# Moving the sums and splits of a third product's weights beside the second product

## The chip, the cores and the metric

One core of a Trainium2 chip runs the kernel, written by hand slot by slot. The metric is device microseconds of one execution (median of the runs shown).

## The reference, cut to what matters

All data are float32. Attention within chunks of 64 tokens makes `x` (4608 x 512); two expert blocks follow, each a product into 2048 columns, an elementwise function and a product back to 512:

```
x = chunked_attention(q, k, v)                      # 4608 x 512
g = relu(x @ w_in1) ** 2;  y = g @ w_out1           # products 1 and 2
h = y @ w_in2
g = where(h >= 1, h, where(h <= -1, 0, (h + 1) ** 2 / 4))   # product 3
out = g @ w_out2                                    # product 4
```

## The kernel before, in words

The weight inputs are 64-bit floats, read as pairs of 32-bit words and decoded to float32 in the kernel. Every operand of a product is split into a high part (a cast to float32r) and a low part (the rest), and each product is three matmuls: high x high, low x high, high x low. Products 2, 3 and 4 and the last part of product 1 use a seven-product scheme (P1 to P7) instead of eight block products. So each weight unit needs: decoding, four sums (`sums`) that turn 4 blocks into 7, a cast (high) and a subtraction (low), after which both are stored to DRAM buffers (`wd`) and loaded later product by product (`load_w`).

The order of all work is written out in slots. A slot is six matmuls of TensorE (PE); `pe_slot` puts matmuls, `at_slot` puts everything else behind them. All engines work through their own instructions in that order, and nearly all DMAs are issued by SyncE (SP) in that order too, so an issue that has to wait holds up all later ones. The stages are: slots 0 to 224 (SX) product 1 of seven of nine token blocks (`plain_h`) with the attention and the weight decoding beside it; slots 224 to 280 (SB1) the last two blocks as seven products (`form_p`); 280 to 560 (SA2) product 2 over five token pairs of 56 slots (`form_b`, w=0); 560 to 840 product 3 (`form_a`); then product 4.

Weight units: 48 units (three matrices m = 0, 1, 2 for products 2, 3 and 4, 16 units each), one begun every 97/20 = 4.85 slots from slot 28 (U0). `stage_unit` loads 512 KB into one of three buffers, `unit_a` (bits, lines 120 to 135) and `unit_b` decode: one ACT and four DVE instructions. For m = 0 and 1 `sums` follows on POOL (4 instructions, line 258), `unit_c` casts on ACT (line 283, tile `wh`, two buffers), `unit_hi` stores, `unit_d` subtracts on DVE (line 292, tile `wl`, two buffers) and stores. For m = 2 the decoded 256 KB go to DRAM (`wq`) and `late_a` to `late_d` load, sum, cast and subtract them beside product 3, 4 units in each pair but the last.

`pair_sums(i)` (line 201, four POOL instructions), `pair_hi` (ACT, line 218) and `pair_lo` (DVE, line 223) do the same for the eight weight pieces that `form_p` uses. `plain_end` squares a result tile `g` of product 1 on POOL (line 619) or ACT and stores it (line 625); `form_p` has four `g` buffers, written by ACT or DVE (line 775). In `form_p`, product P4 of a piece adds onto the bank that DVE reads for P7 (line 775), so its matmuls wait for that read.

Product 2 reads its activations back by `load_g` (line 807, four operands i = 0 to 3 of four parts kp), casts them on ACT (`prep_b`, line 639), subtracts on DVE (line 642) and combines operands on DVE (line 646), 5 slots ahead of PE, with three operand buffers.

Of the kernel before, what the change touches and what calls it, by code (L numbers as in the profile page):

```python
# [8 lines left out]
F32 = mybir.dt.float32  # L9
F32R = mybir.dt.float32r  # L10
U32 = mybir.dt.uint32
AF = mybir.ActivationFunctionType
ALU = mybir.AluOpType
AX = mybir.AxisListType

P = 128
# [18 lines left out]
def chunk_attention_moe_moe2(ctx, tc, q, k, v, w_in1, w_out1, w_in2, w_out2, out):  # L35
# [10 lines left out]
    nc = tc.nc  # L46
# [11 lines left out]
    BLK = 512  # L58
# [3 lines left out]
    NBL = len(blocks)  # L62
# [10 lines left out]
    def f(ap):  # L73
        return ap.bitcast(F32)
# [5 lines left out]
    def qt(tag, shape, dt, name):  # L80

        pool = mp if tag < NQM else late if tag < NQL else mid
        return pool.tile(shape, dt, tag=f"q{tag}", name=name, padded_shape=[P, 2, BLK])

    def ot(tag, n, name):

# [16 lines left out]
        for j in range(NPAIR) for dh in range(2) for th in range(2)  # L103
    }

    wd = {(m, a): dram.tile([P, 2, 2, 7, P], F32, name=f"w{m}_{a}") for m in range(3) for a in range(8)}

    wq = {(a, b): dram.tile([P, 4, P], F32, name=f"q{a}_{b}") for a in range(8) for b in range(2)}

# [151 lines left out]

    def unit_b(m, a, b):
        y, ab = wst[m, a, b]
        if m == 2:
            c = eu.tile([P, 4, P], F32, tag="wl", name="wq", bufs=2, padded_shape=[P, 7, P])
        else:
            c = eu.tile([P, 7, P], F32, tag="wc", name="wc", bufs=1)
        nc.vector.scalar_tensor_tensor(  # L270
            out=c[:, 0:4].rearrange("p a f -> p (a f)"), in0=ab, scalar=TINY, in1=f(y), op0=ALU.is_ge, op1=ALU.mult
        )
        wst[m, a, b] = c
        if m == 2:
            nc.sync.dma_start(out=wq[a, b], in_=c[:, 0:4])
            del wst[m, a, b]
        else:
            sums(c)

    def unit_c(*u):  # L280
        c = wst[u]
        hi = eu.tile([P, 7, P], F32R, tag="wh", name="wh", bufs=2)
        nc.scalar.copy(hi, c)
        wst[u] = (c, hi)

    def unit_hi(m, a, b):
        nc.sync.dma_start(out=wd[m, a][:, 0, b], in_=f(wst[m, a, b][1]))

    def unit_d(m, a, b):
        c, hi = wst.pop((m, a, b))  # L290
        lo = eu.tile([P, 7, P], F32R, tag="wl", name="wl", bufs=2)
        nc.vector.tensor_tensor(out=lo, in0=c, in1=f(hi), op=ALU.subtract)
        nc.sync.dma_start(out=wd[m, a][:, 1, b], in_=f(lo))


    def late_a(a, b):
        c = mp.tile([P, 7, P], F32, tag=f"q{LATE[0]}", name="lc", padded_shape=[P, 8, P])
        nc.sync.dma_start(out=c[:, 0:4], in_=wq[a, b])
        wst[a, b] = c

    def late_b(a, b):
        sums(wst[a, b])

    def late_c(a, b):
        c = wst[a, b]
        hi = mp.tile([P, 7, P], F32R, tag=f"q{LATE[1]}", name="lh", padded_shape=[P, 8, P])
        nc.scalar.copy(hi, c)
        wst[a, b] = (c, hi)

    def late_d(a, b):  # L310
        c, hi = wst.pop((a, b))
        nc.gpsimd.tensor_tensor(out=c, in0=c, in1=f(hi), op=ALU.subtract)
        store_parts(2, a, b, hi, c)

    wt, wv = {}, {}

    def load_w(m, tag, a, prod):
        if tag < 3 * NF:
            t = wp.tile([P, 2, 2, P], F32R, tag=f"w{tag}", name=f"w{m}")
        else:  # L320
            if tag % 2 == 0:
                wv[tag // 2] = wp.tile([P, 2, 2, 2, P], F32R, tag=f"v{tag // 2 - 3 * NF // 2}", name=f"w{m}")
            t = wv[tag // 2][:, tag % 2]
        nc.sync.dma_start(out=f(t), in_=wd[m, a][:, :, :, CIDX[prod]])
        wt[m, a, prod] = t

# [286 lines left out]
    def plain_end(j, fi, g, own):  # L615
        if own:
            nc.scalar.square(g, g)
        else:
            nc.gpsimd.tensor_tensor(out=g, in0=g, in1=g, op=ALU.mult)  # L619
        kh, kk = divmod(fi, HF)  # L620
        b0, n = blocks[j]
        for p, th, t0, m in halves:
            lo, hi = max(b0, t0), min(b0 + n, t0 + m)
            if lo < hi:
                nc.sync.dma_start(out=gd[0, p, kh, th, kk // 2][:, kk % 2, lo - t0:hi - t0], in_=g[:, lo - b0:hi - b0])  # L625
# [305 lines left out]
    with tc.manual_schedule():  # L931
# [150 lines left out]

        units = [(m, a, b) for m in range(3) for a in range(8) for b in range(2)]
        for n, u in enumerate(units):
            g = U0 + n * 97 // 20
            if n < NWS:
                at_slot(U0 - 4 + n, stage_unit, *u)
            at_slot(g, unit_a, *u)
            if n + NWS < len(units):
                at_slot(g, stage_unit, *units[n + NWS])  # L1090
            at_slot(g + 2, unit_b, *u)
            if u[0] < 2:
                at_slot(g + 4, unit_c, *u)
                at_slot(g + 5, unit_hi, *u)
                at_slot(g + 6, unit_d, *u)
        done = g + 7
        assert done <= SB1 - 16, done

# [15 lines left out]


        for i in range(HF):
            s = 165 + 14 * i if i < 3 else SX + 7 * (i - 3) + 7
            at_slot(s, pair_sums, i)
            at_slot(s + 3, pair_hi, i)
            at_slot(s + 4, pair_lo, i)  # L1120
            for prod, o in OFFS.items():
                pe_slot(SX + 7 * i + o, form_p, i, prod)
        m = mid_at
# [39 lines left out]
        for w, s0 in ((0, SB1), (1, SB2)):  # L1163
            for j in range(NPAIR):
                for r, prod in enumerate(RANK):
                    s = s0 + 56 * j + 8 * r
                    for kk in range(HF):
                        pe_slot(s + kk, form_b, w, j, prod, kk)
                    for kp in range(HF // 2):
                        t = s + ((0, 2, 1, 3)[kp] if ended(w, j, prod) else 2 * kp) - PREP  # L1170
                        if j == 0 and r == 0 and w == 0:
                            t = max(t, done + 12)
                        at_slot(t, prep_b, w, j, prod, kp)
                        if prod in AFTER:
                            at_slot(t + 3, comb_b, w, j, prod, kp)
                        if j + 1 < NPAIR:

                            for i, p, d in ((0, "P2", 3), (1, "P3", 3), (3, "P7", 0), (2, "P4", 0)):
                                if p == prod:
                                    at_slot(t + d, load_g, w, j + 1, i, kp)  # L1180
        for kp in range(4):
# [10 lines left out]
        for j in range(NPAIR):  # L1192
            if j == 0:
                e = SA2
                loads = tuple(e - 24 + n for n in range(4))
                times = dict(P1=e - 18, P5=e - 13, P6=e - 8, P3=e - 1, P2=e, P7=e + 1, P4=e + 5)
                combs = (("P1", e - 16, 0), ("P5", e - 11, 0), ("P1", e - 2, 1), ("P2", e + 3, 0))
            else:
                b = SA2 + 7 * (HF * j - 1)
                l0 = SA2 + 7 * (HF * (j - 1) + 2)  # L1200
                loads = tuple(l0 + 7 * n for n in (0, 1, 3, 2))
                times = dict(P1=b - 8, P5=b + 1, P6=b + 5, P3=b + 4, P2=b + 6, P7=b + 7, P4=b + 11)
                combs = (("P1", b - 6, 0), ("P1", b - 5, 1), ("P5", b + 2, 0), ("P2", b + 9, 0))
            for i in range(4):
                at_slot(loads[i], load_xa, j, i, A_RAW[i])
            for prod in sorted(ORD, key=times.get):
                at_slot(times[prod], prep_a, j, prod)
                at_slot(times[prod] + 1, rest_a, j, prod)
            for prod, t, n in combs:
                at_slot(t, comb_a, j, prod, n)  # L1210
            if j + 1 < NPAIR:
                for n in range(4):
                    g = SA2 + 56 * j + 12 + 13 * n
                    u = divmod(4 * j + n, 2)
                    for d, fn in ((0, late_a), (4, late_b), (8, late_c), (9, late_d)):
                        at_slot(g + d, fn, *u)


        for t in range(56):
            r, kk = divmod(t, 8)  # L1220
            i, ro = divmod(t, 7)

            tag = (t + 2 * NF) % 56
            if t < 32:
                s = SX + (23, 30, 37, 44, 51, 58, 65, 45, 9, 11, 16, 18, 30, 44, 58, 29)[t // 2] + t % 2 - 2 * (t < 4)
            else:
                s = SB1 + t - 30
            at_slot(s, load_w, 0, tag, kk, RANK[r])
            two = int(tag >= 3 * NF and tag % 2 == 0)
            at_slot(SB1 + 56 * (NPAIR - 1) + t + t // 2 + two, load_w, 1, tag, i, ORD[ro])  # L1230
            i, ro = divmod(t + two, 7)
            at_slot(SA2 + 7 * (HF * (NPAIR - 1) + i) + OFFS[ORD[ro]] + t // 2, load_w, 2, tag, kk, RANK[r])

        l = SA2 + 7 * (HF * NPAIR - 1)
        for kp in range(4):
# [53 lines left out]
```

## Time and profile before

| | us |
|---|---|
| median of 3 runs | 1589.98 (1589.93 to 1598.41) |
| the profiled execution | 1592.96 |
| its span, first to last instruction | 1591.2 |
| PE busy | 1540.8 (97%) |
| DVE, ACT, POOL busy | 1144.5, 880.1, 337.5 |
| DMA queue of SP | 341.46 MB, 70.9% of 16 engines' span |

The span is what the chain of instructions takes; 1.8 us lie around it. Busy shares are averages over stages with different limits, so a stage is read from the stretch of time in which it runs: `plain_h` until about 440 us, `form_p` until about 538 us, product 2 until about 900 us, product 3 until about 1240 us. PE wait rows say what ended a wait; the granted clock (PEclk) is 1.00 at 2.4 GHz and 0.50 at 1.2 GHz.

### The profile page before, as it was taken

The numbers are of one execution on the slowest core, as the hardware profiler recorded it, in microseconds if no ns is written. First come the engines' busy times: TensorE is split into PE (matmuls) and PEld (weight loads), VectorE is DVE, ScalarE is ACT, GpSimd is POOL, SyncE is SP. The second block draws the span as 40 slices with busy tenths as digits, with TensorE's granted clock in tenths as the row PEclk, the third lists the DMA queues.
The fourth block names the chain that finished last, engine by engine and source line by source line (L and its number), as shares of the span: only waits on it lengthen the run. The fifth ranks groups of instructions, "written<-read, shape, count | busy, mean of one in ns | idle before, by whom it ended". The sixth has DMA issues, their size and how long they took to land.

```text
span 1591.2 us, 26749 instructions
## 1 busy us (share of the span) xinstructions
PE 1540.8 (97%) x9456; PEld 1352.1 (85%) x9456; DVE 1144.5 (72%) x1448; ACT 880.1 (55%) x1785; POOL 337.5 (21%) x382
## 2 busy tenths in 40 slices
PE   7999999989989789999999999999999999999998
PEld 5788888777867668999999888999999889999998
DVE  7977687666696647777776857677575787878876
ACT  6877777666543334444444567667675544444442
POOL 0145555565457200000000022223220000000000
PEclk9999999999999989999999999999999999999999
DMA  9989999999868975336175785655769983744633
GB/s 221 243 269 310 294 294 304 294 298 302 284 194 257 338 218 175 105 127 193 56 241 163 237 295 188 230 189 197 241 219 307 341 220 74 198 112 120 169 75 47
DMA packets 445606, 343.63 MB, mean 216 GB/s; under 512 B 209952, under 2 KB 414752, under 8 KB 445472
## 3 DMA queue, kind: packets, MB, share of 16 engines
q1 hardware_dynamic: 441760, 341.46, 70.9%
q8 instruction: 75, 1.23, 0.3%
q10 hardware_dynamic: 3712, 0.46, 0.2%
q14 instruction: 59, 0.48, 0.1%
HBM read 197.13 MB, written 144.70 MB: 215 GB/s over the span
## 4 chain that ended last, share of the span: by engine, by line
PE 83%; DMA 6%; DVE 4%; issue 2%; SPq 2%; ACT 2%; POOL 2%; POOLq 0%; DVEq 0%; ACTq 0%
PE X L652 37%; PE V L652 18%; PE ph L596 12%; PE W L652 9%; DMA w<-w 2%; PE psA L408 2%; DMA w<-wl 1%; DMA g<-g 1%; PE X L756 1%; PE psD L518 1%; PE psB L431 1%; POOL g L619 1%; PE psC L486 1%; ACT s L449 1%; SPq L625 1%
## 5 line engine op out<-in xcount | busy, mean ns | idle before, releaser
L652 PE MATMUL X<-oh,w 128*128 128x448 f32 (+1 forms) x1920 | 549.0, 367 | 0.0
L639 ACT CAST oh<-gr 128x896 fp32r<-128x896 f32 (+1 forms) x280 | 270.0, 964 | 336.4 <-PE X L652 148.6
L642 DVE TENSOR_TENSOR ol<-gr,oh 128x896 fp32r<-128x896 f32 (+1 forms) x280 | 312.4, 1117 | 166.9 <-ACT oh L639 160.8
L652 PEld LDWEIGHTS X<-oh,w 128*128 128x128 f32 x1920 | 360.1, 188 | 35.8
L652 PE MATMUL X<-ol,w 128*128 128x448 f32 (+1 forms) x960 | 353.2, 368 | 0.4 <-DVE ol L642 0.4
L652 PE MATMUL V<-oh,w 128*128 128x448 f32 (+1 forms) x960 | 276.3, 369 | 12.1 <-DMA w<-w 12.1
L619 POOL TENSOR_TENSOR g<-g 128x512 f32<-128x512 f32 x136 | 169.1, 1247 | 231.4 <-ACT g L608 190.2
L652 PEld LDWEIGHTS V<-oh,w 128*128 128x128 f32 x960 | 180.9, 189 | 31.0 <-issue 11.1
L652 PEld LDWEIGHTS X<-ol,w 128*128 128x128 f32 x960 | 180.1, 188 | 16.7 <-DVE ol L642 0.8
L596 PE MATMUL ph<-xh,ih 128*128 128x512 f32 x448 | 181.6, 405 | 0.0
L646 DVE TENSOR_TENSOR gr<-gr,gr 128x896 f32<-128x896 f32 (+1 forms) x160 | 179.4, 1121 | 1.7 <-DMA gr<-g 1.7
L652 PE MATMUL V<-ol,w 128*128 128x448 f32 (+1 forms) x480 | 177.3, 369 | 0.0
L596 PE MATMUL ph<-xh,il 128*128 128x512 f32 x448 | 175.4, 392 | 1.0 <-DVE il L189 1.0
L596 PE MATMUL ph<-xl,ih 128*128 128x512 f32 x448 | 175.8, 392 | 0.0
L258 POOL TENSOR_TENSOR lc<-lc 128x128 f32<-128x128 f32 x64 | 34.1, 543 | 506.4 <-DMA lc<-q 492.1
L652 PE MATMUL W<-oh,w 128*128 128x448 f32 (+1 forms) x480 | 137.2, 367 | 0.0
L789 ACT ACTIVATE t<-c,half 128x448 f32<-128x448 f32 (+1 forms) x120 | 81.2, 681 | 50.7 <-DVE c L712 49.8
L596 PEld LDWEIGHTS ph<-xl,ih 128*128 128x128 f32 x448 | 84.4, 188 | 18.3
L596 PEld LDWEIGHTS ph<-xh,il 128*128 128x128 f32 x448 | 84.8, 189 | 17.0 <-DVE il L189 1.4
L596 PEld LDWEIGHTS ph<-xh,ih 128*128 128x128 f32 x448 | 84.6, 189 | 16.0 <-ACT g L608 0.5
L652 PEld LDWEIGHTS W<-oh,w 128*128 128x128 f32 x480 | 90.0, 187 | 8.9
L652 PEld LDWEIGHTS V<-ol,w 128*128 128x128 f32 x480 | 90.6, 189 | 8.1
(116 smaller groups left out, 2043.5 us busy)
## 6 DMA issues: line engine op xcount, KB each, us to landing
gr<-g SPq DMA_DIRECT2D x128, 448.0 KB, 4.7
w<-w SPq DMA_DIRECT2D x168, 256.0 KB, 5.1
g<-t SPq DMA_DIRECT2D x128, 224.0 KB, 3.1
wu<-in_moe_w_out_dram SPq DMA_DIRECT2D x64, 256.0 KB, 4.7
gr<-g SPq DMA_DIRECT2D x32, 512.0 KB, 7.0
w<-wh SPq DMA_DIRECT2D x32, 448.0 KB, 4.5
w<-wl SPq DMA_DIRECT2D x32, 448.0 KB, 5.1
ws<-in_moe_w_in_dram SPq DMA_DIRECT2D x16, 512.0 KB, 4.6
```

The lines of the kernel that those rows point to most:

```text
L258: nc.gpsimd.tensor_tensor(out=c[:, o], in0=c[:, x], in1=c[:, z], op=op)
L408: nc.tensor.transpose(pt[:, h // HU, h // 2 % NP, :], qks[t][i][:, h:h + 2, :].rearrange("p h d -> p (h d)"), ident)
L431: nc.tensor.matmul(pt[rows(p), e, c * CH:(c + 1) * CH], qkT[rows(e), 0, p, rows(c)], qkT[rows(e), 1, p, rows(c)], start=True, stop=True,)
L449: nc.scalar.activation(out=s[:, e, c], in_=sc[:, e, c], func=AF.Exp, bias=m[:, e, c:c + 1], accum_out=z[:, e, c:c + 1],)
L486: nc.tensor.transpose(pt[:, e].rearrange("k p t -> k (p t)"), s[:, e, 2 * n:2 * n + 2].rearrange("q c k -> q (c k)"), ident)
L596: nc.tensor.matmul(ph, win[fi][wi][:, kt * P:(kt + 1) * P], x[:, i, :], start=(kt == 0 and a == 0), stop=(kt == KT - 1 and a == 2),)
L619: nc.gpsimd.tensor_tensor(out=g, in0=g, in1=g, op=ALU.mult)
L639: nc.scalar.copy(t[0], raw)
L642: nc.vector.tensor_tensor(out=t[1], in0=raw, in1=f(t[0]), op=ALU.subtract)
L646: eng.tensor_tensor(out=o, in0=x, in1=z, op=ALU.subtract)
L652: nc.tensor.matmul(o, wt_[:, wi, c, :], x[:, i, :], start=first and a == 0, stop=last and a == 2, skip_group_check=True,)
L789: nc.scalar.activation(out=t, in_=h, func=AF.Square, bias=half, scale=0.5)
```

## The change

Seven edits. (1) `unit_b` stops at the decoded blocks for m = 1 too and stores them to `wq`; sums, cast and subtraction become a `late_unit` beside pairs 0 to 3 of product 2, on tiles q16 to q21, q0 and q1 (those of operands 3 and 2 of `load_g`). (2) The loads of operands 3 and 2 for the next pair go 22 slots later in product 2. (3) Units of m = 0 begin every 5 slots, the other 32 every 4.25; the last ends at slot 246 instead of 262, and the first loads of operands 0 and 1, tied to that end, move with it. (4) For m = 0 high and low parts stand side by side in one tile and one DRAM buffer: one store of 896 KB instead of two, and `load_w` reads runs of 1024 instead of 512 bytes. (5) All `pair_sums` are made at slots 112 to 161; casts and subtractions come 3 slots earlier for i >= 3. (6) A `g` tile's store is issued 1 slot (2 in `form_p`) after its square instead of right behind it. (7) The subtraction and the stores of a late unit are separate steps.

```diff
     def unit_b(m, a, b):
-        if m == 2:
-            c = eu.tile([P, 4, P], F32, tag="wl", name="wq", bufs=2, padded_shape=[P, 7, P])
+        if m:
+            c = eu.tile([P, 4, P], F32, tag="wh", name="wq", bufs=2, padded_shape=[P, 14, P])
...
-        if m == 2:
-            nc.sync.dma_start(out=wq[a, b], in_=c[:, 0:4])
+        if m:
+            nc.sync.dma_start(out=wq[m, a, b], in_=c[:, 0:4])
...
     def unit_c(*u):
         c = wst[u]
-        hi = eu.tile([P, 7, P], F32R, tag="wh", name="wh", bufs=2)
+        w = eu.tile([P, 7, 2, P], F32R, tag="wh", name="wh", bufs=2)
+        nc.scalar.copy(w[:, :, 0], c)
...
+    def unit_d(m, a, b):
+        c, w = wst[m, a, b]
+        nc.vector.tensor_tensor(out=w[:, :, 1], in0=c, in1=f(w[:, :, 0]), op=ALU.subtract)
+
+    def unit_e(m, a, b):
+        nc.sync.dma_start(out=wd[m, a][:, b], in_=f(wst.pop((m, a, b))[1]))
...
+    def late_unit(s, u, tags, steps):
+        for d, fn, *args in zip(steps, (late_a, late_b, late_c, late_d, late_e), ((tags,), (), (tags,), (), ())):
+            at_slot(s + d, fn, *u, *args[0])
...
             nc.gpsimd.tensor_tensor(out=g, in0=g, in1=g, op=ALU.mult)
+        at_slot(cur[0] + (2 if j >= NBL - 2 else 1), plain_out, j, fi, g)
...
-            g = U0 + n * 97 // 20
+            g = U0 + 5 * n if n < 16 else U0 + 80 + (n - 16) * 17 // 4
...
-            s = 165 + 14 * i if i < 3 else SX + 7 * (i - 3) + 7
-            at_slot(s, pair_sums, i)
-            at_slot(s + 3, pair_hi, i)
-            at_slot(s + 4, pair_lo, i)
+            s = 166 + 12 * i if i < 3 else SX + 7 * (i - 3) + 7
+            at_slot(112 + 7 * i, pair_sums, i)
+            at_slot(s, pair_hi, i)
+            at_slot(s + 1, pair_lo, i)
...
-                            for i, p, d in ((0, "P2", 3), (1, "P3", 3), (3, "P7", 0), (2, "P4", 0)):
+                            for i, p, d in ((0, "P2", 3), (1, "P3", 3), (3, "P7", 0 if w else 22), (2, "P4", 0 if w else 22)):
...
+        for j in range(4):
+            for n, (d, tags) in enumerate(((29, (16, 17)), (33, (18, 19)), (45, (0, 1)), (49, (20, 21)))):
+                late_unit(SB1 + 56 * j + d, (1, *divmod(4 * j + n, 2)), tags, (0, 5, 8, 9, 11))
```

## Rows read from the trace of the kernel before

**Rows 1.** The page, part 1: busy time of each engine over the span.

```profile
...
PE 1540.8 (97%) x9456; PEld 1352.1 (85%) x9456; DVE 1144.5 (72%) x1448; ACT 880.1 (55%) x1785; POOL 337.5 (21%) x382
...
```

**Rows 2.** Stretches: us, PE, PEld, DVE, ACT, POOL busy, PEclk, DMA share, GB/s.

```profile
...
110.00:300.00 190.00, 189.97 (x1933) 156.96 (x1932) 141.54 (x213) 138.58 (x454) 111.69 (x141) 1.00 0.99 301
300.00:400.00 100.00, 91.14 (x907) 74.81 (x907) 64.49 (x92) 65.27 (x212) 58.29 (x69) 0.97 1.00 299
...
440.00:480.00 40.00, 33.92 (x138) 26.16 (x137) 36.70 (x42) 17.69 (x29) 25.78 (x22) 0.96 0.62 192
480.00:520.00 40.00, 37.25 (x156) 30.06 (x155) 24.30 (x28) 12.57 (x22) 28.43 (x28) 0.96 0.83 261
520.00:540.00 20.00, 15.84 (x64) 12.69 (x63) 10.62 (x10) 6.84 (x9) 8.78 (x6) 0.91 1.00 329
540.00:570.00 30.00, 17.87 (x69) 13.96 (x68) 13.04 (x11) 7.32 (x8) 0.24 (x1) 0.83 1.07 325
...
615.00:683.00 68.00, 68.00 (x335) 62.48 (x335) 49.31 (x50) 30.57 (x36) 0.00 (x0) 1.00 0.42 135
...
920.00:1240.00 320.00, 320.00 (x1571) 294.08 (x1570) 211.53 (x307) 214.00 (x345) 67.78 (x76) 1.00 0.69 234
...
```

**Rows 3.** Waits of PE from 300 to 400 us: total us, times, longest.

```profile
...
PE psD L518 <- ACT atT L505: 4.9, 1, 4.9
PE psC L486 <- ACT g L608: 1.5, 1, 1.5
PE psD L518 <- DMA vt<-in_v_dram: 1.5, 1, 1.5
PE psC L486 <- DVE s L460: 1.0, 1, 1.0
```

**Rows 4.** Waits of PE from 440 to 540 us.

```profile
...
PE X L756 <- DVE g L775: 10.6, 6, 4.2
PE X L756 <- DVE pl L744: 2.0, 1, 2.0
...
```

**Rows 5.** Waits of PE from 540 to 570 us.

```profile
...
PE V L652 <- DMA w<-w: 12.1, 2, 10.7
```

**Rows 6.** Chain that ended last, 525 to 570 us: start, length, what.

```profile
...
529.29 4.81 DMA g<-g
...
534.25 0.70 DVE g L775
...
537.93 8.24 PE X L652 x36
...
558.48 5.41 DMA w<-w
...
```

**Rows 7.** Timeline of ACT, 338.5 to 346 us: start, length, instruction [idle before].

```profile
...
341.70 0.94 ACT L283 CAST wh<-wc 128x896 fp32r<-128x896 f32 x1 [3.46 <-DMA w<-wh]
...
```

**Rows 8.** Groups of POOL, 245 to 520 us: xcount | busy us, mean ns | idle.

```profile
...
L201 POOL TENSOR_TENSOR iy<-iy,iy 128x256 f32<-128x256 f32 x16 | 15.1, 942 | 1.3
...
```

**Rows 9.** Timeline of SP (DMA issues), 530 to 572 us.

```profile
...
541.11 0.42 SPq L807 DMA_DIRECT2D gr<-g  x1
...
550.69 22.21 SPq L324 DMA_DIRECT2D w<-w  x20
```

**Rows 10.** Groups of POOL, 920 to 1240 us.

```profile
...
L312 POOL TENSOR_TENSOR lc<-lc,lh 128x896 f32<-128x896 f32 x16 | 35.5, 2218 | 65.1 <-ACT lh L307 65.1
L258 POOL TENSOR_TENSOR lc<-lc 128x128 f32<-128x128 f32 x60 | 32.3, 549 | 129.2 <-DMA lc<-q 115.0 <-DMA w<-w 11.8
```

**Rows 11.** DMA issues of the whole span: KB each, median us to landing.

```profile
...
gr<-g SPq DMA_DIRECT2D x128, 448.0 KB, 4.7
...
lc<-q SPq DMA_DIRECT2D x16, 256.0 KB, 4.2
...
```

**Rows 12.** The page, part 5: the splitting casts of ACT.

```profile
...
L639 ACT CAST oh<-gr 128x896 fp32r<-128x896 f32 (+1 forms) x280 | 270.0, 964 | 336.4 <-PE X L652 148.6
...
```

**Rows 13.** Line 642 on DVE, 920 to 1240 us: durations ns min/median/max.

```profile
...
L642 DVE TENSOR_TENSOR ol<-xr,oh x28: 1074/1090/1443, 953.1 to 1180.9; 128x896 fp32r<-128x896 f32 x28
...
```

More of the change, by code (lines that the diff above doesn't have):

```diff
@@ L82, in qt @@
         pool = mp if tag < NQM else late if tag < NQL else mid
-        return pool.tile(shape, dt, tag=f"q{tag}", name=name, padded_shape=[P, 2, BLK])
+        return pool.tile(shape, dt, tag=f"q{tag}", name=name, padded_shape=[P, 8, P] if shape[1] == 7 else [P, 2, BLK])
     def ot(tag, n, name):
@@ L104, in chunk_attention_moe_moe2 @@
     }
-    wd = {(m, a): dram.tile([P, 2, 2, 7, P], F32, name=f"w{m}_{a}") for m in range(3) for a in range(8)}
-    wq = {(a, b): dram.tile([P, 4, P], F32, name=f"q{a}_{b}") for a in range(8) for b in range(2)}
+    wd = {
+        (m, a): dram.tile([P, 2, 2, 7, P] if m else [P, 2, 7, 2, P], F32, name=f"w{m}_{a}")
+        for m in range(3) for a in range(8)
+    }
+    wq = {(m, a, b): dram.tile([P, 4, P], F32, name=f"q{m}_{a}_{b}") for m in (1, 2) for a in range(8) for b in range(2)}
     win = {}
@@ L281, in unit_c, with late_a, late_b, late_c @@
         c = wst[u]
-        hi = eu.tile([P, 7, P], F32R, tag="wh", name="wh", bufs=2)
-        nc.scalar.copy(hi, c)
[L284 to L311, printed above, removed]
-        nc.gpsimd.tensor_tensor(out=c, in0=c, in1=f(hi), op=ALU.subtract)
-        store_parts(2, a, b, hi, c)
+        w = eu.tile([P, 7, 2, P], F32R, tag="wh", name="wh", bufs=2)
+        nc.scalar.copy(w[:, :, 0], c)
+        wst[u] = (c, w)
+    def unit_d(m, a, b):
[3 more added lines that the diff above has]
+        nc.sync.dma_start(out=wd[m, a][:, b], in_=f(wst.pop((m, a, b))[1]))
+    def late_a(m, a, b, tags):
+        c = qt(tags[0], [P, 7, P], F32, "lc")
+        nc.sync.dma_start(out=c[:, 0:4], in_=wq[m, a, b])
+        wst[m, a, b] = c
+    def late_b(*u):
+        sums(wst[u])
+    def late_c(m, a, b, tags):
+        c = wst[m, a, b]
+        hi = qt(tags[1], [P, 7, P], F32R, "lh")
+        nc.scalar.copy(hi, c)
+        wst[m, a, b] = (c, hi)
+    def late_d(*u):
+        c, hi = wst[u]
+        nc.gpsimd.tensor_tensor(out=c, in0=c, in1=f(hi), op=ALU.subtract)
+    def late_e(*u):
+        c, hi = wst.pop(u)
+        store_parts(*u, hi, c)
+    def late_unit(s, u, tags, steps):
+        for d, fn, *args in zip(steps, (late_a, late_b, late_c, late_d, late_e), ((tags,), (), (tags,), (), ())):
+            at_slot(s + d, fn, *u, *args[0])
     wt, wv = {}, {}
@@ L323, in load_w @@
             t = wv[tag // 2][:, tag % 2]
-        nc.sync.dma_start(out=f(t), in_=wd[m, a][:, :, :, CIDX[prod]])
-        wt[m, a, prod] = t
+        c = CIDX[prod]
+        nc.sync.dma_start(out=f(t), in_=wd[m, a][:, :, :, c] if m else wd[m, a][:, :, c])
+        wt[m, a, prod] = t if m else t.rearrange("p b h f -> p h b f")
     att, ttile = {}, {}
@@ L619, in plain_end, with plain_out @@
             nc.gpsimd.tensor_tensor(out=g, in0=g, in1=g, op=ALU.mult)
+        at_slot(cur[0] + (2 if j >= NBL - 2 else 1), plain_out, j, fi, g)
+    def plain_out(j, fi, g):
         kh, kk = divmod(fi, HF)
@@ L1091, in chunk_attention_moe_moe2 @@
             at_slot(g + 2, unit_b, *u)
-            if u[0] < 2:
+            if u[0] == 0:
                 at_slot(g + 4, unit_c, *u)
-                at_slot(g + 5, unit_hi, *u)
                 at_slot(g + 6, unit_d, *u)
+                at_slot(g + 7, unit_e, *u)
         done = g + 7
@@ L1214, in chunk_attention_moe_moe2 @@
                     u = divmod(4 * j + n, 2)
-                    for d, fn in ((0, late_a), (4, late_b), (8, late_c), (9, late_d)):
-                        at_slot(g + d, fn, *u)
+                    late_unit(g, (2, *u), LATE, (0, 4, 8, 9, 9))
         for t in range(56):
```

## The prediction

> **What bounds the kernel now.** First the page's busy times: PE is busy 1540.8 us of a span of 1591.2 [rows 1], so 50.4 us of idle time, and what the lower clock costs, are all that a change beside the matmuls can win. Next the stretches [rows 2], to see where the idle time lies: PE is full from 110 to 300 us, from 615 to 683 and from 920 to 1240. It is idle 100 − 91.14 = 8.9 us between 300 and 400, and (40 − 33.92) + (40 − 37.25) + (20 − 15.84) + (30 − 17.87) = 25.1 us between 440 and 570. The remaining 16 us are the start and the tail, which the change does not touch. In the same rows PEclk falls to 0.97, 0.96, 0.96, 0.91 and 0.83: after some waits PE ran at 1.2 instead of 2.4 GHz. Each stretch times (1 − PEclk) gives 3.0, 1.6, 1.6, 1.8 and 5.1 us; where a long wait covers part of it (first and last) I count 2 and 2.5. So 34.0 us of waits and 9.5 us of clock, 43.5 us, is the most to be had. Last the waits themselves [rows 3 to 5] and who made them late.
>
> **Term 1, 300 to 400 us: 10.9 us (8.9 + 2).** The DMA engines are at a share of 1.00 here, as from 110 on at 0.99 [rows 2]. The longest wait, 4.9 us, ends with an ACT copy [rows 3]. ACT had stood 3.46 us before the cast `wh`, until the store of an earlier `wh` had landed [rows 7], with pair sums on POOL following (an instruction of theirs takes 0.94 us, [rows 8], four to a piece). Both leave this stretch. From unit 16 (slot 108) a unit brought 512 KB in and 896 KB out every 4.85 slots, 290 KB per slot; after the change it brings 512 in and 256 out every 4.25 slots, 181 KB per slot. In this stage that is 16 x 640 KB = 10.5 MB less, 35 us of DMA time at the 299 GB/s of the row. Nothing is added to ACT or DVE here, and pair sums take the POOL time that 16 x 4 sums leave. I take 10 won, 0.9 left (bounds: 7, if the three short waits of 4.0 us stay, to 10.9).
>
> **Term 2, the start of `form_p`: 3.6 us (2.0 + 1.6).** PE waits 2.0 us for the low part of P6 [rows 4] and then runs slow. DVE is busy 36.70 of 40 us there [rows 2], and closer units bring no relief: begun before at slots 226, 231, 236, 241, 246, now at 227, 231, 235, 239. What helps is only that operands land earlier when the DMA queue is emptier. Bounds 0 to 3.6; I take 1.6, nearer to nothing.
>
> **Term 3, P4 inside `form_p`: 8.0 us.** Six waits for DVE's read of P7 make 10.6 us [rows 4]; one is term 4 (4.2), 6.4 remain, and one half-speed stretch adds 1.6. DVE came late since POOL did the sums of a piece between squares, ACT's cast and DVE's subtraction waited for the sums, and the `g` stores behind waited on SP. Now sums are long done, ACT and DVE find their input ready, and units end at slot 246, a third of the way into the stage, instead of 262. I take 6.9 won, the first wait staying (bounds 3, if DVE is still full for half the stage, to 8.0).
>
> **Term 4, the last P4: 6.0 us (4.2 + 1.8).** The chain has a `g` store of 4.81 us landing at 534.1, DVE at 534.25, then PE [rows 6]: a store late in a queue with a share of 1.00 [rows 2]. Eight loads of 512 KB (operands 0 and 1) and the last units go about 16 slots earlier, out of this stretch. Against it: a store is now issued 2 slots, 2.7 us, later, and four buffers come round in 7 slots, 9.6 us (36 matmuls take 8.24 us [rows 6], a slot 1.37). The store's way is then 2.7 us + about 2 us of square and issue (estimate) + 3 to 4 us of landing, still under 9.6. I take 5.4 won (bounds 0 to 6.0).
>
> **Term 5, P5's weights in product 2: 14.6 us (12.1 + 2.5).** PE waits for a `load_w` [rows 5] issued 558.48 and landed 563.89 [rows 6]. It is P5's fifth weight: issue slot 289, use slot 292, with eight more 512 KB loads and eleven weight loads before it, and these do not move. The queue starts with the third part of operand 3, issued 541.11 [rows 9]: 3.2 us after the last P4 ended at 537.93 [rows 6], because the store of that P4 stood before it on SP. Now that store comes 2 slots later; ahead stands only the one of P7, whose read and square are done about 1.2 us before P4's end (P7's end, two slots of 1.37, less DVE 0.7, square 1.3 and its turn on SP). So the queue starts 4.4 us earlier. It then takes the same 563.9 − 541.1 = 22.8 us, and 0.8 more for the P4 store that is now inside. Won 3.4 us with the slow clock left, stall 8.7. Larger weight packets could give some 1.5 us more; SP's 22.2 us for 20 issues [rows 9] shows a full ring, but no row shows this load with half the packets, so I count nothing. Bounds 0 to 14.6.
>
> **Term 6, product 2: 0.** A unit costs POOL 4 x 0.549 + 2.218 = 4.4 us [rows 10], so 17.7 us in a pair of 67 us where POOL does nothing now; ACT gets four casts of about 0.96 [rows 12], DVE nothing of its own. DMA gets 16 x 1152 KB = 18.4 MB over 270 us, 68 GB/s on 135, less than the 234 that product 3 bears at PE 320.00 of 320 [rows 2]. Product 3 does 16 such units already. The moved loads of operand 3 go out at slot 49 + 2kp for a combination at 62 + 2kp of the next stage: 13 slots of 1.22 us (335 matmul records in 68 us [rows 2]), 15.8 us, against 4.7 to landing [rows 11]. Late units use these tiles between: load at 29 (landing 4.2 us, [rows 11]), sums at 34, cast at 37, subtraction at 38, store at 40; SP then stands up to 2 us before a store with only loads due 13 slots later behind it. ACT's cast of one unit can wait about 1 us where its sums follow another unit's subtraction on POOL; PE's lead covers that: a buffer comes free 4 slots (4.8 us) ahead of use, and cast 0.96 [rows 12] and subtraction 1.09 [rows 13] leave 2.8 us. Bounds: 0 to +47 us, the fourth rival.
>
> In product 3 nothing moves. In slots 28 to 108 the units of m = 0 come 3% slower with the same bytes in larger pieces, under a PE that is full: 0.
>
> **Sum.** 10 + 1.6 + 6.9 + 5.4 + 3.4 = 27.3 us. From the profiled execution: 1592.96 − 27.3 = 1565.7. That execution was 3.0 us above the median of the runs shown, 1589.98; so I forecast 1589.98 − 27.3 = 1562.7 us.
>
> **The rivals.** (a) *The hand-over clears as well*: the weight loads, in half as many packets, reach P5 in time and `form_p` has no DVE wait. All 43.5 us go: 1546.5. For it: the queue's length is what makes term 5 (share 1.07 [rows 2]); against it: 5 MB that are not urgent stay ahead of the load. (b) *`form_p` keeps its waits*: DVE, not POOL or the stores, sets P4's time, since decoding is as dense as before until slot 241, and stores issued later hold `g` buffers longer. Only terms 1 and 5 are won: 13.4, so 1576.6. For it DVE's 36.70 of 40 [rows 2]; against it 24.30 of 40 in the next 40 us, where waits went on. (c) *The change doesn't empty the queue*: units 14% closer bring loads as fast as stores go; only pair sums help, about 5 us: 1585. Against it the sum of bytes of term 1. (d) *Product 2 becomes bound, slower than before*: POOL holds DVE back for whole instructions. Pairs of late units follow each other on POOL (a subtraction, then the next unit's sums): 4.5 us held, against a lead of 2.8, or 1.7 where a combination of 1.09 stands between. That is 2.8 lost plus 1.7 of half clock, twice in each of four pairs, 36 us; single holds of 2.4 against 1.7 give 0.7 x 16 = 11. With 47 lost against 27.3 won: 1610. It decides once DVE is held over 1.7 us behind POOL. Against it: line 642 beside POOL in product 3 took at most 1.443 us where 1.074 is its least [rows 13], a hold of 0.37, beside POOL instructions of 2.2 us.
>
> The Trainium skill, page "SBUF — State Buffer", section "SBUF: two separate sides", says that VectorE and GpSimd share a port pair as an exclusive lock, that a VectorE instruction with two inputs in SBUF takes part in this, and that the loser blocks for the whole instruction. By that rule rival (d) would be the forecast, and 1610 the time. The trace agrees that there is a hold, and not with its length: 0.37 us, not 2.2.
>
> **How the numbers follow.** The forecast 66% (its own range 1554 to 1571), (a) 14%, (b) 10%, (c) 5%, (d) 5%. The range of 8 in 10 goes from 1549, near (a), to 1578, past (b). A measurement of this kernel tells about 1% (15.9 us, 1574.1) from no change. Faster by more: the forecast, (a) and a part of (b), 85%; within 1%: the rest of (b) and (c), 10%; slower: (d), 5%.
>
> **What would show it.** Right: PE full from 245 to 440 us with a DMA share near 0.85; no wait for DVE's read of P7 longer than 1 us after the first piece; units gone a third into `form_p`; one wait for a weight load of 7 to 10 us early in product 2, with a slow clock behind it; product 2 full with POOL busy a quarter of it. Wrong: PE waits for low parts or casts inside product 2; SP held at `g` stores through `form_p`; a `g` buffer awaited; or the weight wait gone or longer than 12 us.

## The result and the profile after

The changed kernel takes 1602.38 us (median of 9 runs) against 1592.84 us for the kernel before beside it (9 runs): ratio 1.0057, interval 1.0040 to 1.0073. The forecast was 1562.7 with a range of 1549 to 1578. By the prediction's bound of 1% the time is the same, by its interval it is 0.4 to 0.7% slower. One of the nine runs of the changed kernel took 3936.26 us, and ratio and interval leave it out.

The page of the changed kernel, its first line and the busy times: the span grew by 9.2 us, PE is busy 5.4 us longer at the same 9456 matmuls, and POOL has 53.5 us more than in [rows 1].

```profile
span 1600.4 us, 26829 instructions
...
PE 1546.2 (97%) x9456; PEld 1351.9 (84%) x9456; DVE 1144.6 (72%) x1432; ACT 878.6 (55%) x1785; POOL 391.0 (24%) x398
...
```

Stretches of the changed kernel, columns as in [rows 2] (us, PE, PEld, DVE, ACT, POOL busy, PEclk, DMA share, GB/s). The stages lie some 10 to 20 us earlier than before, so they are cut at other times.

```profile
...
300.00:400.00 100.00, 100.00 (x1021) 82.68 (x1019) 61.81 (x101) 69.21 (x237) 41.82 (x41) 1.00 0.92 265
...
432.00:480.00 48.00, 43.85 (x183) 34.78 (x183) 38.85 (x46) 20.47 (x35) 20.34 (x17) 0.96 0.70 226
480.00:530.00 50.00, 46.95 (x200) 38.45 (x199) 24.52 (x25) 16.52 (x25) 21.16 (x17) 0.97 0.85 288
530.00:570.00 40.00, 30.53 (x128) 24.87 (x127) 20.19 (x18) 13.97 (x16) 0.00 (x0) 0.87 0.75 248
...
590.00:900.00 310.00, 292.22 (x1394) 263.56 (x1392) 231.19 (x213) 137.84 (x166) 86.12 (x71) 0.98 0.64 207
920.00:1240.00 320.00, 320.00 (x1566) 293.12 (x1565) 210.00 (x305) 211.63 (x341) 71.29 (x80) 1.00 0.69 233
...
```

The last row is the one to be careful with: product 3 is full in both kernels and carries late units in both. What differs is the row above it: product 2, full before, now leaves PE idle 310 − 292.22 = 17.8 us. In the kernel before PE waited once from 575 to 920 us:

```profile
...
PE X L652 <- DVE ol L642: 0.4, 1, 0.4
```

A landmark splits the difference. PE's wait for P5's fifth weight ends at 564.03 us before (the weight had landed at 563.9, [rows 6]) and here at 544.63, 19.4 us earlier. Timelines of PE, the kernel before and then the changed one:

```profile
...
564.03 1.19 PE L652 MATMUL V<-oh,w 128*128 128x512 f32 x2 [10.74 <-DMA w<-w]
...
544.63 1.19 PE L664 MATMUL V<-oh,w 128*128 128x512 f32 x2 [9.47 <-DMA w<-w]
```

So 19.4 us were won by then, and 19.4 + 9.2 = 28.6 us were lost between there and product 3. The waits of PE in that stretch, 590 to 900 us, say on whom (total us, times, longest):

```profile
...
PE V L664 <- DVE ol L654: 6.4, 4, 1.6
PE X L664 <- DVE ol L654: 6.4, 8, 1.6
PE V L664 <- ACT oh L651: 4.5, 4, 1.1
PE X L664 <- ACT oh L651: 0.5, 2, 0.3
```

They are 17.8 us for casts (line 651, line 639 before) and subtractions (line 654, 642 before) of product 2's operands. Two low-clock stretches add about 6.5 us (PEclk 0.68 from 620 to 630 us and 0.67 from 770 to 780). Each begins about two waits of 1.1 and 1.6 us close together; at two other such pairs (694 and 844 us) the clock stayed at 1.00. The rest, some 4 us by difference, no row resolves.

The row that names the cause belongs to ACT, in its waits from 590 to 900 us: ACT stands before the late cast until POOL's sums are done.

```profile
...
ACT lh L308 <- POOL lc L261: 43.8, 13, 4.8
...
```

How it happens is seen in one pair. First the issues of SP and what POOL and ACT do from 674 to 694 us; the third late unit's load goes out at 675.18, in a burst of two late stores, two `y` stores, three operand loads and two late loads:

```profile
...
674.07 0.55 SPq L264 DMA_DIRECT2D w<-lh  x1
674.71 0.38 SPq L265 DMA_DIRECT2D w<-lc  x1
675.18 0.89 SPq L299 DMA_DIRECT2D lc<-q  x1
676.16 1.88 SPq L882 DMA_DIRECT2D y<-c  x2
678.09 0.52 SPq L819 DMA_DIRECT2D gr<-g  x1
678.73 0.82 SPq L299 DMA_DIRECT2D lc<-q  x1
679.59 2.25 SPq L819 DMA_DIRECT2D gr<-g  x2
...
```

POOL begins the sums at 681.71, when that load has landed, 6.5 us after its issue:

```profile
...
681.71 2.57 POOL L261 TENSOR_TENSOR lc<-lc 128x128 f32<-128x128 f32 x4 [11.24 <-DMA lc<-q]
685.33 2.12 POOL L313 TENSOR_TENSOR lc<-lc,lh 128x896 f32<-128x896 f32 x1 [1.05 <-DMA lc<-q]
687.40 5.11 POOL L261 TENSOR_TENSOR lc<-lc 128x128 f32<-128x128 f32 x4
...
```

ACT, whose order has the late cast (line 308) ahead of product 2's next casts, waits for each set of sums:

```profile
...
679.39 0.94 ACT L651 CAST oh<-gr 128x896 fp32r<-128x896 f32 x1 [1.46 <-PE X L664]
684.31 0.94 ACT L308 CAST lh<-lc 128x896 fp32r<-128x896 f32 x1 [3.98 <-POOL lc L261]
...
686.01 1.79 ACT L651 CAST oh<-gr 128x896 fp32r<-128x896 f32 x2
692.54 0.94 ACT L308 CAST lh<-lc 128x896 fp32r<-128x896 f32 x1 [4.75 <-POOL lc L261]
...
```

Two casts in a row at 686.01 are the sign of a queue held up: normally each is released by PE, as at 679.39. The 2.8 us that the prediction counted as PE's lead do not cover 4.0 and 4.75. One link more is in these rows: ACT stood ready for the third unit's cast at 684.31 − 3.98 = 680.33, only 5.2 us after that unit's load was issued, where the order gives 8 slots, 9.8 us. The load itself went out late. An operand load ahead of it on SP, issued at 671.45, had waited until 671.42 for a combination on DVE (the one of 3.01 us shown below).

POOL's groups from 590 to 900 us answer to [rows 10]: a sum takes 0.926 us in the mean where it took 0.549 beside product 3. DVE and POOL hold each other up. The four sums at 681.71, with DVE idle from 682.46 on, took 2.57 us; the four at 687.40 took 5.11, and the four instructions of DVE beside them 1.34 to 1.41 each instead of 1.08.

```profile
...
L261 POOL TENSOR_TENSOR lc<-lc 128x128 f32<-128x128 f32 x56 | 51.3, 926 | 151.1 <-DMA lc<-q 104.7 <-issue 44.2
L313 POOL TENSOR_TENSOR lc<-lc,lh 128x896 f32<-128x896 f32 x15 | 35.1, 2342 | 18.8 <-ACT lh L308 17.8 <-DMA lc<-q 1.1
```

DVE's longest holds come beside POOL's subtraction (line 313) and not beside the sums. The same combination (line 658) takes 1.35 us at the end of POOL's sums, then 3.01 us beside the subtraction that POOL began at 667.59 (timelines of DVE and of POOL):

```profile
...
666.14 1.35 DVE L658 TENSOR_TENSOR gr<-gr,gr 128x896 f32<-128x896 f32 x1
...
668.41 3.01 DVE L658 TENSOR_TENSOR gr<-gr,gr 128x896 f32<-128x896 f32 x1
...
667.59 2.87 POOL L313 TENSOR_TENSOR lc<-lc,lh 128x896 f32<-128x896 f32 x1 [1.06 <-ACT lh L308]
...
```

Two theories stood: A, ACT's queue is held by a cast that comes before its input; B, POOL holds DVE (the forecast's rival d).

### The profile page after: what moved, and what is told of

Same layout as the page of the kernel before. It is cut to its first block, busy times and chain, and to the rows that moved or that the text cites. A ratio compares the mean times of both kernels' runs of the same rounds, so it can differ in the third digit from the quotient of the medians.

```text
span 1600.4 us, 26829 instructions
## 1 busy us (share of the span) xinstructions
PE 1546.2 (97%) x9456; PEld 1351.9 (84%) x9456; DVE 1144.6 (72%) x1432; ACT 878.6 (55%) x1785; POOL 391.0 (24%) x398
## 5 line engine op out<-in xcount | busy, mean ns | idle before, releaser
L654 DVE TENSOR_TENSOR ol<-gr,oh 128x896 fp32r<-128x896 f32 (+1 forms) x280 | 322.6, 1154 | 169.5 <-ACT oh L651 166.9
L664 PE MATMUL V<-oh,w 128*128 128x448 f32 (+1 forms) x960 | 279.9, 373 | 13.9 <-DMA w<-w 9.5
L628 POOL TENSOR_TENSOR g<-g 128x512 f32<-128x512 f32 x136 | 164.6, 1213 | 275.3 <-ACT g L617 194.9
L664 PEld LDWEIGHTS X<-ol,w 128*128 128x128 f32 x960 | 180.1, 188 | 28.6 <-DVE ol L654 11.6
L658 DVE TENSOR_TENSOR gr<-gr,gr 128x896 f32<-128x896 f32 (+1 forms) x160 | 194.1, 1213 | 1.8 <-DMA gr<-g 1.8
L261 POOL TENSOR_TENSOR lc<-lc 128x128 f32<-128x128 f32 x128 | 92.8, 735 | 417.7 <-DMA lc<-q 356.7
L617 ACT ACTIVATE g<-ph 128x512 f32<-128x512 f32 x112 | 67.7, 604 | 58.4 <-PE ph L605 30.5
```

Source lines behind the costliest of these rows:

```text
L261: nc.gpsimd.tensor_tensor(out=c[:, o], in0=c[:, x], in1=c[:, z], op=op)
L617: nc.scalar.activation(out=g, in_=ph, func=AF.Relu)
L654: nc.vector.tensor_tensor(out=t[1], in0=raw, in1=f(t[0]), op=ALU.subtract)
L658: eng.tensor_tensor(out=o, in0=x, in1=z, op=ALU.subtract)
L664: nc.tensor.matmul(o, wt_[:, wi, c, :], x[:, i, :], start=first and a == 0, stop=last and a == 2, skip_group_check=True,)
```

## The experiments

**The late cast, subtraction and stores 4 slots later.**

```diff
-                late_unit(SB1 + 56 * j + d, (1, *divmod(4 * j + n, 2)), tags, (0, 5, 8, 9, 11))
+                late_unit(SB1 + 56 * j + d, (1, *divmod(4 * j + n, 2)), tags, (0, 5, 12, 13, 15))
```

> The changed kernel with the cast, subtraction and stores of the third product's late units 4 slots later (steps 0, 5, 12, 13, 15 instead of 0, 5, 8, 9, 11). Theory A (ACT's queue is held): the 43.8 us that ACT stands before a late cast until POOL's sums are done (16 units, up to 4.8 us each) delay the casts of product 2's operands behind it; 4 slots are 4.9 us, so the waits go, product 2 is full again, and the time is about 1602 - 25 = 1577 us. Theory B (POOL holds DVE): subtractions and combinations beside POOL are as slow as before, PE's waits for line 654 stay, time within 4 us of 1602.

Measured: 1578.13 us, ratio to before 0.9923 (0.9904 to 0.9943), as A expected. Waits of PE, 590 to 900 us, fall from 17.8 to 4.4 us:

```profile
...
PE V L664 <- DVE ol L654: 3.0, 4, 0.8
PE X L664 <- DVE ol L654: 1.4, 3, 0.6
```

ACT's wait for the sums in the same stretch:

```profile
...
ACT lh L308 <- POOL lc L261: 2.7, 2, 2.0
...
```

And B is answered by line 654 itself. Durations (ns min/median/max) in the changed kernel, 590 to 900 us:

```profile
...
L654 DVE TENSOR_TENSOR ol<-gr,oh x116: 1076/1093/2270, 590.6 to 899.5; 128x896 fp32r<-128x896 f32 x111, 128x1024 fp32r<-128x1024 f32 x5
...
```

and in this run:

```profile
...
L654 DVE TENSOR_TENSOR ol<-gr,oh x116: 1074/1092/3142, 590.1 to 874.3; 128x896 fp32r<-128x896 f32 x112, 128x1024 fp32r<-128x1024 f32 x4
...
```

Line 658, the combination, is no better off. Groups of DVE, 590 to 900 us, in the changed kernel and then in this run:

```profile
...
L658 DVE TENSOR_TENSOR gr<-gr,gr 128x896 f32<-128x896 f32 x64 | 80.7, 1260 | 0.0
...
L658 DVE TENSOR_TENSOR gr<-gr,gr 128x896 f32<-128x896 f32 x64 | 86.5, 1352 | 0.0
...
```

DVE is held longer here (line 654 at worst 3.14 instead of 2.27 us, line 658 on average 1.352 instead of 1.260), yet PE waits a quarter as long. The hold of DVE is real, but most of the time lost is not its doing.

**Late units as traffic alone.** The sums, cast and subtraction of the third product's late units are left out (so the third product has wrong weights); the same bytes are loaded and stored.

```diff
     def late_b(*u):
-        sums(wst[u])
+        if u[0] == 2:
+            sums(wst[u])
...
+        m, a, b = u
+        for w in range(2):
+            nc.sync.dma_start(out=wd[m, a][:, w, b, 0:4], in_=c[:, 0:4])
+            nc.sync.dma_start(out=wd[m, a][:, w, b, 4:7], in_=c[:, 0:3])
```

> The changed kernel, the late units of the third product loaded and stored with the same bytes but without their four sums, cast and subtraction (these are left out, so the third product's weights are not the right ones). Theories A and B alike: no engine has late work in product 2, PE is full there, about 1602 - 28 = 1574 us. Rival C (the DMA bursts of late loads, stores and moved operand loads delay product 2's operands): PE's waits stay for the most part, 1590 us or more.

Measured: 1569.96 us, ratio 0.9871 (0.9847 to 0.9894). PE's waits from 560 to 900 us (in this kernel lines 664 and 654 are 674 and 664):

```profile
...
PE X L674 <- DVE ol L664: 0.4, 1, 0.4
```

Product 2 is as full as in the kernel before, which had the same wait of 0.4 us. The DMA traffic of the late units alone costs nothing, so rival C falls. Against the first run, 1578.13 − 1569.96 = 8 us are left for late work on the engines when ACT is hardly held any more: at most that is the size of B, since ACT's own late casts are in it.

**The pair sums and the spaced stores alone, in the kernel before.**

```diff
-            s = 165 + 14 * i if i < 3 else SX + 7 * (i - 3) + 7
-            at_slot(s, pair_sums, i)
-            at_slot(s + 3, pair_hi, i)
-            at_slot(s + 4, pair_lo, i)
+            s = 166 + 12 * i if i < 3 else SX + 7 * (i - 3) + 7
+            at_slot(112 + 7 * i, pair_sums, i)
+            at_slot(s, pair_hi, i)
+            at_slot(s + 1, pair_lo, i)
...
+        at_slot(cur[0] + (2 if j >= NBL - 2 else 1), plain_out, j, fi, g)
```

> The kernel before with two edits of the change alone: all pair sums at slots 112 to 161 with casts and subtractions 3 slots earlier, and the stores of g tiles spaced by 1 or 2 slots. If the order on POOL and SP made most of the waits before product 2: about 12 us less than before, 1581 us. If the bytes of the units' stores made them: at most 4 us less, 1589 us or more.

Measured: 1588.88 us, ratio 0.9993 (0.9983 to 1.0002): nothing that can be measured. With the third product's splits still in the first stage the waits for the most part change places: 28.5 us in all from 240 to 570 us, against 34.0 before, with new ones for ACT. (The traces compared are of executions of 1587.13 and 1592.96 us, further apart than the medians.) PE's waits, 240 to 570 us (lines 655 and 759 are lines 652 and 756 of the kernel before):

```profile
...
PE V L655 <- DMA w<-w: 9.6, 1, 9.6
PE psD L518 <- ACT atT L505: 6.6, 3, 3.0
PE X L759 <- ACT sp L769: 5.5, 2, 4.9
...
```

**The same two edits taken out of the first run's kernel.**

```diff
-            at_slot(112 + 7 * i, pair_sums, i)
-            at_slot(s, pair_hi, i)
-            at_slot(s + 1, pair_lo, i)
+            at_slot(s, pair_sums, i)
+            at_slot(s + 3, pair_hi, i)
+            at_slot(s + 4, pair_lo, i)
...
-        at_slot(cur[0] + (2 if j >= NBL - 2 else 1), plain_out, j, fi, g)
+        plain_out(j, fi, g)
```

> The first run's kernel with the pair sums, casts and subtractions back at their old slots and the g stores right behind the squares. If the deferred bytes make what is won before product 2: 3 us more than the first run at most, 1581 us or less. If the order on POOL and SP has a large part: 8 us or more above the first run, 1586 us or more.

Measured: 1587.33 us, ratio 0.9968 (0.9955 to 0.9982), 9 us above the first run (0.9923). So the two edits are worth nothing while the splits are in the first stage, and 7 to 9 us once they are gone. The gain before product 2 cannot be shared out edit by edit, but the trace tells it by stage. With the two edits taken out PE stays nearly full from 300 to 400 us (columns as in [rows 2]), while its waits for DVE's read of P7 are twice those of the first run, 8.5 us against 4.3:

```profile
...
300.00:400.00 100.00, 98.99 (x996) 81.82 (x988) 63.03 (x100) 68.04 (x237) 43.30 (x40) 1.00 0.89 257
...
```

So the deferral by itself filled the end of product 1, and the two edits act in `form_p`.

**The old spacing of the units, in the first run's kernel.**

```diff
-            g = U0 + 5 * n if n < 16 else U0 + 80 + (n - 16) * 17 // 4
+            g = U0 + n * 97 // 20
```

> The first run's kernel with all units 97/20 slots apart as before. If ending the units early is what empties the DMA queue before product 2: waits return at the end of form_p and the time is 5 us or more above the first run, 1583 us or more. If the bytes alone do: within 3 us of 1578.

Measured: 1580.64 us, ratio 0.9926 (0.9902 to 0.9951), not to be told from 0.9923. Ending the units 16 slots earlier gives nothing that can be measured here. The half of the expectation that is about waits came true: in `form_p` (430 to 540 us) PE waits 5.0 us for ACT copies, where the first run has 0.6, and less for DVE's read of P7, 2.7 us instead of 4.3.

**P5's weight first.** In the changed kernel.

```diff
-            s = SX + (23, 30, 37, 44, 51, 58, 65, 45, 9, 11, 16, 18, 30, 44, 58, 29)[t // 2] + t % 2 - 2 * (t < 4)
+            s = SX + (23, 30, 37, 44, 51, 58, 56, 45, 9, 11, 16, 18, 30, 44, 58, 29)[t // 2] + t % 2 - 2 * (t < 4)
...
-            at_slot(SB1 + 4, load_g, 0, 0, 2, kp)
+            at_slot(SB1 + 18 + 2 * kp, load_g, 0, 0, 2, kp)
```

> The changed kernel with the load of P5's fifth and sixth weight 9 slots earlier (slots 280 and 281 instead of 289 and 290) and the four loads of operand 2 of the first pair at slots 298 to 304 instead of 284. If the order of the queue makes the 9.5 us wait at the start of product 2: the wait and its slow clock go, 1602 - 12 = 1590 us. If the bandwidth does: the wait moves to another weight load, 1598 us or more.

Measured: 1590.31 us, ratio 0.9995 (0.9984 to 1.0007), against 1.0057 for the changed kernel: 10 us. In PE's waits from 430 to 570 us no weight is left:

```profile
...
PE X L768 <- DVE g L787: 4.8, 3, 3.1
...
```

The order of the queue made that wait, not its bandwidth.

**Only the subtraction and the stores 4 slots later** (steps 0, 5, 8, 13, 15), in the changed kernel.

```diff
-                late_unit(SB1 + 56 * j + d, (1, *divmod(4 * j + n, 2)), tags, (0, 5, 8, 9, 11))
+                late_unit(SB1 + 56 * j + d, (1, *divmod(4 * j + n, 2)), tags, (0, 5, 8, 13, 15))
```

> The changed kernel with only the subtraction and the stores of the late units 4 slots later (steps 0, 5, 8, 13, 15); the cast keeps its slot. If ACT's cast before POOL's sums is what costs: the first and third unit of each pair hold ACT as before (2 to 4 us each), the second and fourth less, since their sums no longer stand behind a subtraction on POOL; about half of the first run's 25 us, 1590 us. If the subtractions beside DVE's work cost: nearly all of it, 1580 us.

Measured: 1594.72 us, ratio 1.0025 (1.0012 to 1.0038): 8 us under the changed kernel by medians (5 by the ratios), not the 12 expected of A and far from the other theory. ACT's wait for sums, 570 to 900 us:

```profile
...
ACT lh L308 <- POOL lc L261: 31.4, 8, 4.4
...
```

**The second and fourth unit of a pair 8 slots behind the one before**, the cast at its old step, in the changed kernel.

```diff
-            for n, (d, tags) in enumerate(((29, (16, 17)), (33, (18, 19)), (45, (0, 1)), (49, (20, 21)))):
+            for n, (d, tags) in enumerate(((29, (16, 17)), (37, (18, 19)), (45, (0, 1)), (53, (20, 21)))):
```

> The changed kernel with the second and fourth late unit of a pair begun 8 slots behind the one before instead of 4 (29, 37, 45, 53), the cast at its old step. If two units on top of each other on POOL cost: their hold of ACT falls from 4.7 us to that of the others, about 1588 us. If the late landing of the loads costs: the holds stay at 4 us each, 1598 us or more.

Measured: 1577.52 us, ratio 0.9920 (0.9902 to 0.9939), better than either theory's number: all of the first run's gain with the cast where it was. ACT's wait for sums:

```profile
...
ACT lh L308 <- POOL lc L261: 11.3, 7, 4.1
...
```

In the pair from 640 to 700 us the third unit's load now lands in 5.2 us instead of 6.4, and ACT stands 0.3 us before that unit's cast instead of 4.0: with the units apart the other holds fell too. The three ways of shortening the same wait line up: 43.8 us of it at 1602.4, 31.4 at 1594.7, 11.3 at 1577.5, 2.7 at 1578.1. The last two cost the same: most of 11.3 us is inside PE's lead (PE's waits from 560 to 900 us are 3.0 us in all).

**Both corrections together** (the cast and what follows it 4 slots later; P5's weight first, with the diff shown there).

```diff
-            at_slot(SB1 + 4, load_g, 0, 0, 2, kp)
+            at_slot(SB1 + 18 + 2 * kp, load_g, 0, 0, 2, kp)
...
-                late_unit(SB1 + 56 * j + d, (1, *divmod(4 * j + n, 2)), tags, (0, 5, 8, 9, 11))
+                late_unit(SB1 + 56 * j + d, (1, *divmod(4 * j + n, 2)), tags, (0, 5, 12, 13, 15))
```

> The late cast 4 slots later (first run) and P5's weight first (fourth run) together. If the two losses are independent, ACT's queue in product 2 and the order of the DMA queue at its start: 1590.7 - 12.6 - 12.1 = 1566 us (the first run gained 12.6 on before, the fourth 12.1 on the changed kernel). If the one hides the other: 1572 us or more.

Measured: 1567.79 us, ratio 0.9843 (0.9815 to 0.9871), near the 1566 of the sum. They add up.

**And the first loads of operands 0 and 1 spread.**

```diff
-                at_slot(done + 1 + 5 * n + kp, load_g, 0, 0, i, kp)
+                at_slot(done + 1 + 12 * n + 3 * kp, load_g, 0, 0, i, kp)
```

> As the kernel with both, and the eight loads of operands 0 and 1 of product 2's first pair 3 slots apart over slots 247 to 268 instead of in two bursts at 247 to 255. If those bursts hold up the stores of the g tiles and so the 3.1 us wait in the middle of the form_p stage: the wait and its slow clock go, 4 to 5 us less than the kernel with both, 1561 us. If the stores issued 2 slots later make the wait: the same time, 1566 us.

Measured: 1564.59 us, ratio 0.9821 (0.9797 to 0.9846). The two intervals overlap, but the wait itself is settled by its row. DVE's longest hold of P4 was 3.1 us in the changed kernel; here, from 430 to 570 us:

```profile
...
PE X L768 <- DVE pl L756: 2.2, 2, 1.6
PE X L768 <- DVE g L787: 1.3, 2, 1.1
...
```

DVE's waits for the store of an earlier `g` tile fell with it. The kernel with both, then this one, 430 to 530 us:

```profile
...
DVE g L787 <- DMA g<-g: 9.9, 4, 4.3
...
DVE g L787 <- DMA g<-g: 4.3, 3, 1.9
...
```

So bursts of 512 KB loads, not the later stores alone, kept `g` buffers from coming free.

**And the cast of the first matrix's units one slot later beside product 1.**

```diff
-                at_slot(g + 4, unit_c, *u)
+                at_slot(g + 5, unit_c, *u)
```

> The kernel with the late cast, P5's weight first and the loads spread, and the cast of the first matrix's units one slot later beside the first product (5 slots after the unit's start instead of 4). If ACT held before POOL's sums also makes the three waits at 115, 162 and 207 us (3.0 us): they go, about 1562 us against 1564.6. If not, the same.

Measured: 1563.74 us, ratio 0.9828 (0.9810 to 0.9845). The three waits before 300 us are gone from the trace, in place of

```profile
...
PE psD L527 <- ACT atT L514: 3.0, 3, 1.6
```

in the changed kernel (PE's waits, 66 to 300 us). The time cannot be told from the run before it (0.9821). This version and that one are the fastest: about 1.7% under the kernel before and 38 us under the changed one.

## Why the prediction was wrong

The sum had six terms. Five were about what the change wins before product 2, and they came out at 19.4 us for 27.3. The sixth, product 2, was put at 0 and cost 28.6.

**Term 6 failed, at the step "ACT's cast of one unit can wait about 1 us where its sums follow another unit's subtraction on POOL; PE's lead covers that".** The wait was 43.8 us over 13 of the casts counted, up to 4.8 us against the lead of 2.8. The step used three durations from calmer places: a load landing in 4.2 us [rows 11] took 6.5 in the burst that the moved operand loads and late stores make of that stretch; four sums at 0.549 [rows 10] took 0.926 each, up to 5.1 us a set; and the second unit's sums begin behind the first one's subtraction. Each came from a known row, none of them measured beside product 2. And the late issue on SP of each pair's third load was not in the sum at all: ACT stood ready for its cast 4.9 to 6.0 us after the issue, not 9.8. The runs confirm it from three sides (cast later, subtraction later, units apart).

**Rival (d) had the place and the sign and the wrong engine.** It priced POOL holding DVE and decided "once DVE is held over 1.7 us". DVE was held by 1.9 us (3.01 instead of 1.08), well over the 0.37 that [rows 13] showed beside product 3; so that row did not carry over either. But the first run, with DVE held even longer, lost most of the waits. The cost of late work on the engines when ACT is hardly held is at most 8 us, of the 47 of the rival. Of the Trainium skill's rule in "SBUF — State Buffer", section "SBUF: two separate sides", that the loser of the shared ports blocks for a whole instruction, the trace of the changed kernel shows more than the kernel before did: 1.9 us over the usual 1.08, beside a subtraction of POOL that took 2.87 us.

**Term 1** (10 of 10.9 forecast): PE is full from 300 to 400 us, at a DMA share of 0.92 and not the 0.85 expected; right as to mechanism, 10.9 won. With the deferral done the pair sums had little part in it (PE busy 98.99 of 100 us with them back). Not foreseen: three waits of 3.0 us earlier on, before 210 us, from ACT's cast of the first matrix standing before its sums, the same fault in small; the last run removes them.

**Term 2** (1.6 of 3.6): the wait is 2.6 us instead of 2.0 and the low clock still follows. Nothing was won, the lower bound. DVE was still busy 38.85 of 48 us.

**Terms 3 and 4** (6.9 and 5.4): of 10.6 us for DVE's read of P7, 4.2 are left, 3.1 of them at once, with one low-clock stretch (PEclk 0.97 from 480 to 530 us). By PE's waits of the changed kernel, 430 to 530 us:

```profile
...
PE X L768 <- DVE g L787: 4.2, 2, 3.1
PE X L768 <- DVE pl L756: 2.6, 1, 2.6
...
```

The loads that term 4 moved out of the last slots arrived as a burst in the middle of the stage and delayed the `g` stores there. Rival (b) had named a later store; the spread loads show that the burst was what it needed.

**Term 5** (stall 8.7 left of 12.1): 9.5 us, right in mechanism and within 0.8 us in size, the size in part by luck. The queue was to start 4.4 us earlier against PE and to take 23.6 us to the weight. Its first issue came 1.14 us after PE had left the last P4 (522.53 and 521.39, by the timelines of SP and PE) instead of 3.38 (541.11 and 537.73), so 2.2 us earlier; and from there to PE's start took 22.1 us (to 544.63) where it took 22.9 before. The two errors go against each other. Of the 12.1 us, moreover, 1.4 were another weight's wait, so P5's own fell from 10.7 to 9.5. P5's weight first shows that the order of the queue, which the change left alone, is the cause.

With term 6 put right (first run) the time is 1578.13, just past the edge of the range, and 12.6 us are won on 1590.7 instead of 27.3. Of what is missing, 4.4 us are waits left in product 2. Terms 1 to 5 fell 8 us short in the changed kernel; the larger parts are 3.0 in the three early waits and some 6 in terms 2 to 4, which were to win 13.9. There the rows show 6.4 us less of waits for DVE's read of P7, 0.6 us more of term 2's wait, and one low-clock stretch less (1.7 us).

## What to carry to other kernels

An in-order engine must not meet a moved instruction before its input is there: place it by the input's worst arrival in its new surroundings, and take every duration of that chain (the load's landing, the neighbour engine's instruction) from rows of the stage it goes to, or else from the worst row. A deferred task is cheap if its steps are spread, and costly if two of them stand on top of each other in front of an engine that feeds PE. When loads are moved out of a stretch, ask for whose stores they land beside next.

## What the runs showed that was not expected

DVE and POOL slow each other far more beside product 2 than beside product 3: a combination of 1.08 us took 3.01 beside a subtraction of POOL, and a sum of 0.55 took 0.93. Why product 3 bears the same pairing with holds of 0.37 is not shown. The two edits on sums and stores were worth 0.9993 alone and 7 to 9 us after the deferral, so their worth depends on which wait ends last. And traffic of some 19 MB added to product 2 cost PE nothing: in the run with traffic alone PE waited 0.4 us in all.
